# The norms' sum over partitions as one bfloat16 product instead of a float32 product

## The chip, the cores and the metric

The kernel runs on one core of a Trainium2 chip. The metric is the device time of one execution in microseconds. Before the change it was 866.14 us, the median of three runs (863.68 to 867.47).

## The reference

A random-feature attention (batch 8, 8 heads, 576 tokens, head size 64, 128 features) is followed by a bilinear feed-forward block. Cut to what matters:

```python
def phi(x):                       # x scaled by 1/sqrt(sqrt(D))
    h = einsum('bhsd,md->bhsm', x, omega) - sum(x * x, -1, keepdims=True) / 2
    return exp(h - max(h, -1, keepdims=True)) / sqrt(m)
q_p, k_p = phi(q_s), phi(k_s)
kv  = einsum('bhsm,bhsd->bhmd', k_p, v)
z   = sum(k_p, axis=2)
out = einsum('bhsm,bhmd->bhsd', q_p, kv) / (einsum('bhsm,bhm->bhs', q_p, z)[..., None] + 1e-6)
x   = out.transpose(0, 2, 1, 3).reshape(B * S, H * D)
y   = ((x @ w1) * (x @ w2)) @ w3 @ w_out
```

Everything is float32 at the interface.

## The kernel before, in words

The 4608 tokens are handled in 36 chunks of 128 tokens. Large products are done in split float16: an operand is scaled by a power of two and split into a high and a low half, and three products (high by high, high by low, low by high, the list `PASSES`) take the place of one float32 product. The power of two for a split comes from a norm, and the norms are what the change touches.

**A norm** has three steps. ScalarE squares a block and adds each partition's row up into one column of a small float32 tile (`square_sum`, L160: `sums` for the q and k chunks, `vam` for a batch of v, `wam` for W, `om_sq` for omega). TensorE multiplies this tile with a 128 by 128 matrix of ones, so that each partition holds the sum over all partitions (`power_of_two`, L165, one PSUM bank `norm_...`, 1, 3 or 8 columns). VectorE takes the exponent bits of this sum (L175), makes a power of two (L178), and its reciprocal (L180). ScalarE and VectorE then use the two to scale and split (`qhl`, `khl`, `vhl`: L143, L146).

**The stages.** For about the first 290 us the weights arrive as 64-bit words, are turned to float32 by VectorE (L500 to L504), W is made as a product of w3 and w_out (`wp`, L574 and L576), and w1, w2 and W are split. The first chunks of k and q (KF = 9 and QF = 5 of them) are projected straight in float32 (`kpj`, `qpj`, L276), the others by split float16 (L283). From then on a steady rhythm runs per chunk: the projection of q and k (`qpj`, `kpj`, L283), the attention product of a chunk (`nu`, L401), per batch the sum over keys (`kvp`, L366), the gated products (`ab`, L636, two weights, 256 tokens at a time), and the output product (`o`, L665). Every chunk of q and k that is split has one norm for both; every batch has one for v.

**What sets the order.** The order in which the parts are written comes from `step`, `put` and the loop over slots at the end (norms three slots ahead of a chunk, scale two, split one), with gate and output products taken from a queue one per slot. The framework then assigns each instruction to its engine, and every engine works through its own list in order. A line of the framework's list is one instruction; on the chip one float32 product runs as two weight loads and two matmul records, a float16 or bfloat16 product as one of each.

The matrix of float32 ones is the tile `ones` (L125, L126); a bfloat16 matrix of ones, `ones_bf` (L123, L124), already exists for the column sums of the weights' magnitudes (`l1s`, L528).

Of the kernel before, what the change touches and what calls it, by code (L numbers as in the profile page):

```python
# [9 lines left out]
F32 = mybir.dt.float32  # L10
F16 = mybir.dt.float16
BF16 = mybir.dt.bfloat16
# [7 lines left out]
P = 128  # L20
# [48 lines left out]
def tile_favor_attention_then_bilinear_ffn(  # L69
# [19 lines left out]
    nc = tc.nc  # L89
# [15 lines left out]
    const = ctx.enter_context(tc.tile_pool(name="const", bufs=1))  # L105
# [9 lines left out]
    def bank_m(name):  # L115
        return ps_m.tile([P, 512], F32, tag="pm", name=name)

    def small(name, n=1, rows=P, dt=F32, bufs=4):
        return sm.tile([rows, n], dt, tag=f"s_{name}", name=name, bufs=bufs)
# [2 lines left out]
    make_identity(nc, ident)  # L122
    ones_bf = const.tile([P, P], BF16, name="ones_bf")  # L123
    nc.vector.memset(ones_bf, 1.0)  # L124
    ones = const.tile([P, P], F32, name="ones")  # L125
    nc.vector.memset(ones, 1.0)  # L126
    ln_e = const.tile([P, 1], F32, name="ln_e")
    nc.vector.memset(ln_e, 15 * math.log(2.0))

# [32 lines left out]
    def power_of_two(cols, n, name, pre=1.0, add=False, bufs=4):  # L162

        bank = bank_m(f"norm_{name}")
        nc.tensor.matmul(bank[:, 0:n], ones, cols, start=True, stop=True)  # L165
        t = bank[:, 0:n]
        if add:
            total = small("total")
            nc.vector.tensor_reduce(total, t, AX.X, ALU.add)
            t, n = total, 1  # L170

        q = bank[:, 16 : 16 + n]
        p = bank[:, 32 : 32 + n]

        nc.vector.tensor_scalar(  # L175
            q.bitcast(I32), t.bitcast(I32), 24, 23, ALU.logical_shift_right, ALU.logical_shift_left
        )
        nc.vector.tensor_scalar(p, q, 2.0**50 / pre, 2.0**-77 / pre, ALU.mult, ALU.max)  # L178
        s = small(f"s{n}_{bufs}", n, bufs=bufs)
        nc.vector.reciprocal(s, p)  # L180
        return p, s
# [17 lines left out]
    om_sq = const.tile([P, 1], F32, name="om_sq")  # L199
    square_sum(om_sq, om_raw, "om")  # L200
    pom, som = power_of_two(om_sq, 1, "om")
    nc.scalar.mul(om[:, 0], om_raw, som)
    nc.vector.scalar_tensor_tensor(om[:, 1], om_raw, som, om[:, 0], ALU.mult, ALU.subtract)
# [29 lines left out]
    def scale(keys, am):  # L233
        p, s = power_of_two(am, 3, "_".join(f"{a}{c}" for a, c in keys), QK_PRE)
        es = small("es", 3)
        nc.vector.tensor_scalar(es, p, unom, None, ALU.mult)
        for i, k in enumerate(keys):
            scales[k] = s[:, i : i + 1], es[:, i : i + 1]
# [102 lines left out]
    def v_scale(b):  # L341
        p, sv[b] = power_of_two(vam[b], 8, f"v{b}", add=True, bufs=3)
        pv[b] = small("pv", bufs=4)
        nc.vector.tensor_scalar_mul(pv[b], p, 2.0**10)
# [370 lines left out]
    for ch in ORDER:  # L715
        n = seen.get(ch, 0)
# [95 lines left out]
    for t in range(max(plan) + 1):  # L812
        n = min(PER[t] if t < len(PER) else 1, len(ticks))
# [9 lines left out]
        n = max([1] + [-(-(k + 1) // max(due[b] - t, 1)) for k, (b, _) in enumerate(v_work)])  # L823
# [43 lines left out]
```

## Time and profile before

| what | value |
|---|---|
| median of three runs | 866.14 us |
| the profiled execution | 866.7 us |
| its span in the trace | 865.0 us |
| TensorE matmul busy | 789.3 us, 91% |
| TensorE weight loads busy | 585.1 us, 68% |
| VectorE busy | 594.4 us, 69% |
| ScalarE busy | 455.0 us, 53% |
| GpSimd busy | 222.0 us, 26% |

The span is the stretch of the trace from the first to the last instruction; 1.7 us of the profiled execution lie around it. A busy share is an average over stages, so the stage has to be looked at before an engine is called the bound. Matmuls are pipelined: the duration of one record holds its way through the array, so the cost of a product in a dense stream is read from the distance between starts, not from its duration.

### The profile page before, as it was taken

The numbers are of one execution on the slowest core, as the hardware profiler recorded it, in microseconds if no ns is written. First come the engines' busy times: TensorE is split into PE (matmuls) and PEld (weight loads), VectorE is DVE, ScalarE is ACT, GpSimd is POOL, SyncE is SP. The second block draws the span as 40 slices with busy tenths as digits, with TensorE's granted clock in tenths as the row PEclk, the third lists the DMA queues.
The fourth block names the chain that finished last, engine by engine and source line by source line (L and its number), as shares of the span: only waits on it lengthen the run. The fifth ranks groups of instructions, "written<-read, shape, count | busy, mean of one in ns | idle before, by whom it ended". The sixth has DMA issues, their size and how long they took to land.

```text
span 865.0 us, 20229 instructions
## 1 busy us (share of the span) xinstructions
PE 789.3 (91%) x8479; PEld 585.1 (68%) x8484; DVE 594.4 (69%) x1066; ACT 455.0 (53%) x813; POOL 222.0 (26%) x220
## 2 busy tenths in 40 slices
PE   2876399489996899999999999999999999999998
PEld 2344255387875777777777777877777777777774
DVE  5778887887879877777877777778777754652200
ACT  2667566758456665655565656555655443322221
POOL 0000010222333433334333334343333342222110
PEclk9996599699998999999999999999999999999999
DMA  8455646432444643644534434335342343332100
GB/s 328 150 191 164 196 129 190 119 59 62 87 112 102 96 115 95 98 75 98 123 86 87 111 98 99 74 89 133 87 87 62 62 80 81 63 62 49 37 14 36
DMA packets 142522, 88.40 MB, mean 102 GB/s; under 512 B 116704, under 2 KB 116832, under 8 KB 142432
## 3 DMA queue, kind: packets, MB, share of 16 engines
q1 hardware_dynamic: 134944, 66.15, 33.7%
q10 hardware_dynamic: 7488, 20.97, 7.3%
q8 instruction: 66, 1.08, 0.5%
q14 instruction: 24, 0.20, 0.1%
HBM read 49.35 MB, written 9.44 MB: 68 GB/s over the span
## 4 chain that ended last, share of the span: by engine, by line
PE 81%; DVE 8%; DMA 4%; ACT 4%; issue 2%; POOL 0%; SPq 0%; ACTq 0%; DVEq 0%
PE ab L636 40%; PE o L665 20%; PE wp L576 7%; PE nu L401 3%; PE kvp L366 3%; PE qpj L283 2%; PE kpj L283 2%; DMA kraw<-kT 1%; DVE nm L295 1%; DMA eqT<-eq 1%; PE wp L574 1%; DMA qraw<-qT 1%; DVE w12b L504 1%; DVE arena L503 1%; PE kpj L276 1%
## 5 line engine op out<-in xcount | busy, mean ns | idle before, releaser
L636 PE MATMUL ab<-xT,w12b 128*128 128x256 f16 (+1 forms) x3840 | 396.0, 263 | 10.4 <-DMA xT<-xhl 7.1
L636 PEld LDWEIGHTS <-w12b 128*128 128x128 f16 x3840 | 342.7, 99 | 51.7 <-issue 9.0
L665 PE MATMUL o<-Wb,arena 128*128 128x512 f16 x864 | 193.6, 379 | 1.1 <-DVE Wb L146 0.6
L651 POOL TENSOR_TENSOR arena<-asb,arena 128x512 f16<-128x512 f32 x72 | 84.5, 1174 | 294.9 <-ACT arena L650 294.4
L665 PEld LDWEIGHTS <-arena 128*128 128x128 f16 x864 | 84.3, 100 | 94.6 <-issue 1.5
L318 POOL TENSOR_TENSOR eq<-qe,eq 128x1024 f16<-128x1024 f32 x34 | 73.9, 2172 | 141.2 <-DVE eq L132 86.8
L646 DVE TENSOR_TENSOR asb<-ab,asb 128x512 f32<-128x512 f32 x72 | 49.4, 687 | 62.9 <-PE ab L636 62.5
L650 ACT CAST arena<-asb 128x512 f16<-128x512 f32 x72 | 44.3, 615 | 85.5 <-DVE asb L646 85.5
L318 POOL TENSOR_TENSOR ek<-ke,ek 128x1024 f16<-128x1024 f32 x28 | 59.7, 2131 | 103.2 <-ACT ek L134 62.2
L576 PE MATMUL wp<-w12b 128*128 128x512 f32 x128 | 60.9, 631 | 13.5 <-DVE w12b L504 13.5
L309 ACT ACTIVATE qe<-qe,ln_e,es 128x1024 f32<-128x1024 f32 x31 | 38.4, 1240 | 47.6 <-DVE qe L308 47.6
L146 DVE SCALAR_TENSOR_TENSOR khl<-kraw,s,khl 128x512 f16<-128x512 f32 x27 | 49.3, 1827 | 16.2 <-ACT khl L143 16.2
L576 PEld LDWEIGHTS wp<-w12b 128*128 128x128 f32 x128 | 25.6, 203 | 45.7 <-issue 31.3
L309 ACT ACTIVATE ke<-ke,ln_e,es 128x1024 f32<-128x1024 f32 x27 | 33.5, 1241 | 42.9 <-DVE ke L308 42.9
L146 DVE SCALAR_TENSOR_TENSOR qhl<-qraw,s,qhl 128x512 f16<-128x512 f32 x31 | 27.9, 899 | 37.7 <-ACT qhl L143 37.7
L401 PEld LDWEIGHTS <-eqT 128*128 128x128 f16 (+1 forms) x960 | 32.4, 101 | 29.0 <-DMA eqT<-eq 19.4
L401 PE MATMUL nu<-kv,eqT 128*128 128x65 f16 (+1 forms) x960 | 34.8, 196 | 18.5 <-DMA eqT<-eq 18.5
L160 ACT ACTIVATE junk_q<-qraw 128x512 bf16<-128x512 f32 x31 | 19.5, 630 | 60.4 <-DMA qraw<-qT 60.4
L645 ACT ACTIVATE asb<-ab 128x512 f32<-128x512 f32 x72 | 42.0, 584 | 16.1 <-PE ab L636 11.0
L437 ACT ACTIVATE xhl<-xs,p2r 128x512 f16<-128x512 f32 x36 | 25.9, 719 | 41.1 <-DVE p2r L189 40.1
L295 DVE TENSOR_REDUCE nm<-kpj 128x8 f32<-128x1024 f32 x36 | 43.8, 1217 | 3.6 <-PE kpj L276 3.3
L132 DVE CAST eq<-qe 128x1024 f16<-128x1024 f32 x31 | 21.5, 693 | 34.2 <-ACT qe L309 34.2
(127 smaller groups left out, 996.2 us busy)
## 6 DMA issues: line engine op xcount, KB each, us to landing
kraw<-kT SPq DMA_DIRECT2D x36, 256.0 KB, 2.7
vraw<-v SPq DMA_DIRECT2D x36, 256.0 KB, 3.5
qraw<-qT SPq DMA_DIRECT2D x36, 256.0 KB, 2.7
out<-o SPq DMA_DIRECT2D x36, 256.0 KB, 2.2
arena<-w3T ACTq DMA_DIRECT2D x8, 1024.0 KB, 5.2
arena<-w ACTq DMA_DIRECT2D x8, 1024.0 KB, 6.0
arena<-wo ACTq DMA_DIRECT2D x4, 1024.0 KB, 6.1
eqT<-eq SPq DMA_TRANSPOSE x72, 3.1
```

The costliest lines, as they stand in the source:

```text
L146: nc.vector.scalar_tensor_tensor(lo, src, s, hi, ALU.mult, ALU.subtract)
L295: nc.vector.tensor_reduce(nm, pj, AX.X, ALU.max, negate=True)
L309: nc.scalar.activation(e, e, AF.Exp, scale=es, bias=ln_e)
L318: (nc.vector if lo == "d" else nc.gpsimd).tensor_tensor(t[:, 1], e, t[:, 0], ALU.subtract)
L401: nc.tensor.matmul(nu[r0:r1, h // 4, h % 4], t[:, x, place(h), r0:r1], kvs[b][:, y, h], start=n == 0, stop=n == 2,)
L576: nc.tensor.matmul(ps, w[:, j, k * P : (k + 1) * P], guest[:, j], start=j == j0, stop=j == HALF - 1,)
L636: nc.tensor.matmul(ps[:, k], w12[m][i][cc][:, a, r * P : (r + 1) * P], x[:, b, cc, off : off + T], start=j == 0, stop=j == len(mm) - 1,)
L645: nc.scalar.mul(asb, ab[0], 2.0**-37)
L646: nc.vector.tensor_tensor(asb, ab[1], asb, ALU.mult)
L650: nc.scalar.copy(h[:, 0], asb)
L651: nc.gpsimd.tensor_tensor(h[:, 1], asb, h[:, 0], ALU.subtract)
L665: nc.tensor.matmul(ps, hs[c, f][0][:, a], W[f][:, b], start=i == 0, stop=i == len(mm) - 1)
```

## The change

The float32 matrix `ones` and its memset are gone. The sum over partitions in `power_of_two` is now a product with `ones_bf`, and the other operand is the float32 tile read as bfloat16, every second element from the second on: the upper 16 bits of each float32 word. The lower 16 bits of the sums are left out of the sum.

```diff
     ones_bf = const.tile([P, P], BF16, name="ones_bf")
     nc.vector.memset(ones_bf, 1.0)
-    ones = const.tile([P, P], F32, name="ones")
-    nc.vector.memset(ones, 1.0)
...
         bank = bank_m(f"norm_{name}")
-        nc.tensor.matmul(bank[:, 0:n], ones, cols, start=True, stop=True)
+        nc.tensor.matmul(bank[:, 0:n], ones_bf, cols.bitcast(BF16)[:, 1::2], start=True, stop=True)
```

Line numbers of the changed kernel are two lower from there on. The lists of ScalarE, GpSimd and SyncE have the same instructions in the same order; VectorE's lacks the one memset. TensorE's has one more instruction at each of the 42 norms, since a bfloat16 product is written as a weight load and a matmul.

TensorE in the steady rhythm, where the norm of q chunk 13 and k chunk 18 stands between the last projection product of a k chunk and the output products; before:

```order
L283 LDWEIGHTS khl_17_4111
L283 MATMUL kpj_17_4288<-om_87,khl_17_4111 128x128
L165 MATMUL norm_q13_k18_4321<-sums_1_103,ones_80 128x3
L665 LDWEIGHTS arena_111
L665 MATMUL o_6_4335<-Wb_84,arena_111 128x512
```

and with the change:

```order
L281 LDWEIGHTS khl_17_4109
L281 MATMUL kpj_17_4286<-om_85,khl_17_4109 128x128
L163 LDWEIGHTS ones_bf_78
L163 MATMUL norm_q13_k18_4319<-sums_1_101,ones_bf_78 128x3
L663 LDWEIGHTS arena_109
L663 MATMUL o_6_4333<-Wb_82,arena_109 128x512
```

The place in the list is the same; the one row has become two.

TensorE at the start, where the norm of omega stands among the eight float32 products of the first k chunk; before:

```order
L862 UNCONDITIONAL_BRANCH
L276 MATMUL kpj_0_139<-Wb_84,kraw_0_114 128x128 x3
L165 MATMUL norm_om_91<-om_sq_88,ones_80 128x1
L276 MATMUL kpj_0_139<-Wb_84,kraw_0_114 128x128 x5
L276 MATMUL kpj_1_209<-Wb_84,kraw_1_116 128x128 x8
```

and with the change:

```order
L860 UNCONDITIONAL_BRANCH
L274 MATMUL kpj_0_137<-Wb_82,kraw_0_112 128x128 x3
L163 LDWEIGHTS ones_bf_78
L163 MATMUL norm_om_89<-om_sq_86,ones_bf_78 128x1
L274 MATMUL kpj_0_137<-Wb_82,kraw_0_112 128x128 x5
L274 MATMUL kpj_1_207<-Wb_82,kraw_1_114 128x128 x8
```

Here too the place is the same. Besides the norms, two neighbouring pairs have changed places in TensorE's list: two `ab` products with each other, and four `ab` products with one `kvp` product of the same batch.

## Rows read from the trace of the kernel before

**Rows 1.** Windows: us, then busy of each engine, granted clock, DMA share, GB/s.

```profile
90.00:100.00 10.00, 1.88 (x14) 1.49 (x14) 9.91 (x12) 8.11 (x18) 0.00 (x0) 0.50 0.48 117
...
289.00:400.00 111.00, 111.00 (x1342) 87.05 (x1343) 84.31 (x153) 63.35 (x107) 40.78 (x44) 0.98 0.49 99
```

**Rows 2.** TensorE's waits from 289 us to the end.

```profile
PE kvp L366 <- DVE ke L308: 2.8, 1, 2.8
```

**Rows 3.** Instructions on the tile `ones`: durations min/median/max, first and last start.

```profile
L165 PE MATMUL norm_q_k<-sums,ones x52: 168/252/273, 202.6 to 672.0; 128*128 128x3 f32 x52
...
L126 DVE MEMSET ones<- x1: 165/165/165, 1.0 to 1.0; 128x128 f32 x1
```

**Rows 4.** TensorE in order of time, in pieces: start, us, what.

```profile
305.61 0.84 PE L283 MATMUL kpj<-om,khl 64*128 64x128 f16 x24
306.39 0.38 PE L165 MATMUL norm_q_k<-sums,ones 128*128 128x3 f32 x2
306.63 3.61 PE L665 MATMUL o<-Wb,arena 128*128 128x512 f16 x16
...
348.80 0.90 PE L401 MATMUL nu<-kv,eqT 128*128 128x65 f16 x24
349.54 5.41 PE L636 MATMUL ab<-xT,w12b 128*128 128x256 f16 x48
354.88 0.84 PE L283 MATMUL qpj<-om,qhl 64*128 64x128 f16 x24
355.65 5.41 PE L636 MATMUL ab<-xT,w12b 128*128 128x256 f16 x48
...
367.93 3.79 PE L366 MATMUL kvp<-vhl,ek 128*128 128x65 f16 x120
...
407.85 0.90 PE L401 MATMUL nu<-kv,eqT 128*128 128x65 f16 x24
...
408.81 5.40 PE L636 MATMUL ab<-xT,w12b 128*128 128x256 f16 x48
...
690.28 0.38 PE L165 MATMUL norm_q<-sums,ones 128*128 128x3 f32 x2
```

**Rows 5.** The same view late: `ab` to `o` with (norm left out) and without a norm.

```profile
702.55 5.41 PE L636 MATMUL ab<-xT,w12b 128*128 128x256 f16 x48
...
707.94 5.34 PE L665 MATMUL o<-Wb,arena 128*128 128x512 f16 x24
...
776.10 5.41 PE L636 MATMUL ab<-xT,w12b 128*128 128x256 f16 x48
781.35 5.34 PE L665 MATMUL o<-Wb,arena 128*128 128x512 f16 x24
```

**Rows 6.** The chain that ended last, before 290 us, in order of time: start, us, what.

```profile
8.34 0.52 PE norm_om L165 x2
...
105.29 8.79 PE wp L576 x16
...
115.17 7.06 PE wp L576 x16
122.24 5.36 PE ab L636 x96
...
136.97 0.20 PE norm_v L165 x2
...
180.26 0.17 PE norm_k L165 x2
...
223.73 0.12 PE norm_q_k L165 x2
```

**Rows 7.** The same chain later: the `kvp` products of one batch.

```profile
368.09 3.63 PE kvp L366 x120
```

**Rows 8.** Weight loads of bfloat16 ones: shape, count, busy us, mean ns, idle before.

```profile
L528 PEld LDWEIGHTS <-ones_bf 128*128 128x128 bf16 x16 | 1.3, 110 | 1.3 <-issue 1.0
```

**Rows 9.** VectorE in order of time: the reading that sets a `kpj` bank free.

```profile
364.00 1.23 DVE L308 TENSOR_TENSOR ke<-kpj,nm 128x1024 f32<-128x1024 f32 x1
```

## The prediction

> **What bounds the kernel now.** The windows by stage come first. From 90 to 100 us TensorE is busy for 1.88 of 10 us at a granted clock of 0.50, while VectorE is busy for 9.91; from 289 to 400 us TensorE is busy for all of 111 us, VectorE for 84.31 and ScalarE for 63.35 [rows 1]. So there are two kernels in one: before about 290 us a chain that goes from engine to engine, after it one in which TensorE does not rest. The waits confirm the second: from 289 us to the end TensorE waits once, for 2.8 us, and this is the wait for the `kvp` products that opens the stretch [rows 2]. Whatever TensorE does not have to do after it is time won, as long as the other engines keep up; before it, only what lies on the chain counts.
>
> Next comes what a norm costs there, and a record's duration misleads. The 26 joint norms of q and k alone are 52 matmul records with a median of 252 ns [rows 3]; that is the way through the array, much of which lies beside the neighbours. I therefore compare the distance between the starts of what stands before and behind, with a norm and without.
>
> - Between `kpj` and `o`: from the first `kpj` to the first `o` it is 306.63 - 305.61 = 1.02 us; the equal 24 products of `qpj` hand over to `ab` after 355.65 - 354.88 = 0.77 us without a norm [rows 4]. The norm costs 0.25 us. This happens 21 times, first with the norm at 306.39 us and last with that at 690.28 us [rows 4].
> - Between `nu` and `ab`: 408.81 - 407.85 = 0.96 us with the norm of v, 349.54 - 348.80 = 0.74 us without [rows 4]. It costs 0.22 us, 5 times.
> - Between `ab` and `o`, late, where only q is left: 707.94 - 702.55 = 5.39 us with, 781.35 - 776.10 = 5.25 us without [rows 5]. It costs 0.14 us, 4 times: the longer `ab` products cover part of the float32 weight load.
>
> Together 21 x 0.25 + 5 x 0.22 + 4 x 0.14 = 6.9 us of the dense stretch are norms. The other 12 of the 42 norms stand before 290 us, and four of them show on the chain: 0.52, 0.20, 0.17 and 0.12 us [rows 6], together 1.0 us.
>
> **The change part by part.** *The float32 product goes.* This takes away 6.9 us after 290 us and at most 1.0 us before.
>
> *A bfloat16 pair comes in its place*, one weight load and one product of at most 8 columns. No row shows such a pair among others. The nearest are pairs of the same full weight load with a float16 product of 65 columns: 120 `kvp` products take 3.63 us [rows 7], so 30 ns for a pair. I take 0.03 us for each of the 30, 0.9 us in all. The bounds: nothing, since a pair inserted in a full stream cannot take less; and 0.11 us, a whole weight load of bfloat16 ones laid bare [rows 8], 3.3 us in all. The 30 ns are nearer because the load in the `kvp` stream has as little cover as here.
>
> A pair with a longer product is dearer: 96 `ab` products of 128 columns take 5.36 us, 56 ns for a load and a product [rows 6]. Against my price stands the Trainium skill, page "TensorE: Matmul & The Clock Gate", section "Back-to-back issue gap": a stream of weight loads and products of 128 columns is said to sustain about 81 ns for a pair. This case's trace does not agree, with 56 ns for the same pair. By the page's figure an estimate for the new pairs is 30 x 0.081 = 2.4 us, and the whole gain would be 5.0 us instead of the 6.5 us below.
>
> *The dense stretch* wins 6.9 - 0.9 = 6.0 us, with bounds of 3.6 and 6.9.
>
> *The stretch before 290 us.* The norm of omega is the one that matters: its 0.52 us lie straight on the chain, between the first float32 `kpj` and VectorE's work on the first weights. The other three are short, and transfers and waits behind them may swallow what they give. With new pairs of 0.03 us, and 0.06 us for the first, at most 1.0 - 0.15 = 0.85 us are won. I take 0.5 us, about what the norm of omega gives, and keep 0 and 0.85 as ends.
>
> *The result comes sooner*, by some tenths of a microsecond. I count nothing for it in the dense stretch, where no TensorE work waits for VectorE [rows 2].
>
> *The memset goes*, 165 ns at 1.0 us [rows 3]; the first norm starts at 8.34 us [rows 6], so its cover is wide, and without it the cost would be those 165 ns once. The truncated sums may turn a power of two by one step now and then; no instruction depends on its value. *The two exchanged pairs* of TensorE's list move products of 30 to 56 ns past each other before 290 us; nothing.
>
> *Nothing new is waited for.* The pair waits for the squares as the float32 product did. What is queued behind it on TensorE (`o` or `ab`) starts sooner; it reads operands made a step earlier. What is late next is a PSUM bank: `kvp` at 367.93 us takes the bank that VectorE sets free at 364.00 + 1.23 = 365.23 us [rows 4, 9], 2.7 us ahead, and the change brings TensorE forward by about 0.2 us in a step of 18 us, with VectorE at three quarters of its time.
>
> **Sum.** 6.0 + 0.5 = 6.5 us. The profiled execution took 866.7 us (a span of 865.0 and 1.7 around it), so it would take 860.2 us. The median of the runs is 0.56 us lower, 866.14 us, and becomes **859.6 us**, 0.75% less.
>
> **The rivals.**
>
> 1. *The pair costs more than 30 ns*, since its load and the load behind it find only a product of a few columns to hide beside. At the 56 ns of an `ab` pair [rows 6] 30 of them cost 1.7 us, the gain is 6.9 - 1.7 + 0.5 = 5.7 us and the time 860.4 us; with a whole load of 0.11 us bare and nothing won early it is 3.6 us and 862.5 us. For it speaks that no row has a bfloat16 pair so short; against it, that even the long float32 loads are partly covered behind `ab`. The page named above lies between the two, at 861.1 us.
> 2. *The early stretch takes a different turn.* TensorE's clock is granted at 0.50 (1.2 GHz, the lower of its two levels) where it stood still most [rows 1]. Sixteen equal `wp` products took 8.79 us when they began behind such a wait and 7.06 us a little later [rows 6]: 1.7 us for one burst more at the lower level. One burst gives 861.3 us, two 863.0; one less gives 857.9. For it: shifts of tenths before 100 us reach a clock that changes there; against it: no wait there hangs on a norm for longer than 0.5 us.
> 3. *The gain is swallowed by another engine*, 866.1 us. Against it stand the 2.7 us of slack and VectorE's 84.31 us of 111 [rows 1, 9].
> 4. *Slower: the stream drains at each change of type.* If the bfloat16 load could begin only once the float16 products had left the array, and the next float16 load only once the norm had left it, load, product and next load would stand in series: 0.11 + 0.25 + 0.11 = 0.47 us with the durations of [rows 3, 8], 14.1 us for 30 against 6.9 removed, and 873.3 us with nothing won early. It turns into a loss from 0.23 us a norm. Against it: the float32 norm is such a change of type too, and costs 0.14 to 0.25 us with two loads and two products.
> 5. *The list promises one load and one product, the chip makes two of each as for float32.* Then nothing changes, 866.1 us. Against it: the bfloat16 ones for the weights' magnitudes have 16 loads for 16 listed products [rows 8].
>
> **How the numbers follow.** My forecast 0.58; the dearer pair 0.20, most of it below 861.8 us; the early stretch 0.10; swallowed 0.08; slower 0.03; two of each 0.01. A measurement of this kernel can tell about 0.5%, or 4.3 us, from no change: faster is below 861.8 us. The runs before lie up to 2.5 us from their median, so about a tenth of the forecast's own chance falls above that line, as do four tenths of the dearer pair, half of the early turn and the swallowed gain. Faster 0.69, within 0.5% 0.28, slower 0.03. The range: the free pair with all of the early gain gives 866.14 - 6.9 - 0.85 = 858.4 us, and a little over a microsecond for the scatter of a median leads to 857.2; upward it takes in the bare load and reaches 863.4.
>
> **What would show it.** Right: 42 matmul records and 42 weight loads on the norm's line instead of 84 each; 0.80 us in place of 1.02 from the first `kpj` to the first `o`, and about 5.28 in place of 5.39 from `ab` to `o`; TensorE without waits after its dense stretch has begun; that stretch about 6 us shorter, and its begin less than 1 us earlier. Wrong: new TensorE waits in it (rival 3), a distance from `kpj` to `o` above 0.85 us (rival 1) or above 1.0 us (rival 4), or a begin of the stretch that moved by more than 1 us either way (rival 2).

## The result and the profile after

The changed kernel takes 858.09 us in the median of five runs (856.64 to 861.15), against 866.14 us before. The ratio is 0.9914 with a 95% interval of 0.9886 to 0.9943, a gain of 7.4 us (4.9 to 9.9). A second measurement of the same kernel (`again`, below) gives 859.03 us and a ratio of 0.9929 (0.9910 to 0.9948), a gain of 6.1 us (4.5 to 7.8). Forecast were 859.6 us and a gain of 6.5.

The windows of the changed kernel, with the columns of [rows 1]:

```profile
90.00:100.00 10.00, 1.88 (x14) 1.49 (x14) 8.52 (x11) 6.42 (x15) 0.00 (x0) 0.50 0.67 181
289.00:400.00 111.00, 111.00 (x1296) 84.78 (x1293) 84.42 (x150) 61.35 (x103) 40.25 (x45) 1.00 0.48 97
```

There are still two stages: TensorE without a pause in the dense stretch and at 1.88 of 10 us near 95 us. VectorE has 84.42 us of 111, so no engine has come close to the bound. TensorE's waits from 275 us to the end, which answer to [rows 2]:

```profile
PE kvp L364 <- DVE ke L306: 2.9, 1, 2.9
PE kpj L281 <- DVE khl L144: 1.6, 1, 1.6
```

Only the opening wait lies in the dense stretch; the other stood before it already, outside the window of [rows 2]. No new wait has come. The instructions on `ones_bf` at the norms, which answer to [rows 3]:

```profile
L163 PEld LDWEIGHTS <-ones_bf x42: 95/96/105, 8.2 to 753.7; 128*128 128x128 bf16 x42
L163 PE MATMUL norm_q_k<-sums,ones_bf x26: 167/178/178, 199.0 to 662.5; 128*128 128x3 bf16 x26
```

For 26 joint norms there are 26 matmul records where there were 52, and 42 weight loads in all where there were 84. TensorE in order of time, which answers to [rows 4, 5]:

```profile
301.04 0.84 PE L281 MATMUL kpj<-om,khl 64*128 64x128 f16 x24
301.82 0.18 PE L163 MATMUL norm_q_k<-sums,ones_bf 128*128 128x3 bf16 x1
301.86 5.34 PE L663 MATMUL o<-Wb,arena 128*128 128x512 f16 x24
307.03 0.90 PE L399 MATMUL nu<-kv,eqT 128*128 128x65 f16 x24
307.77 0.17 PE L163 MATMUL norm_v<-vam,ones_bf 128*128 128x8 bf16 x1
307.80 2.45 PE L634 MATMUL ab<-xT,w12b 128*128 128x256 f16 x21
...
692.76 5.41 PE L634 MATMUL ab<-xT,w12b 128*128 128x256 f16 x48
698.01 0.17 PE L163 MATMUL norm_q<-sums,ones_bf 128*128 128x3 bf16 x1
698.04 5.34 PE L663 MATMUL o<-Wb,arena 128*128 128x512 f16 x24
```

This is where the time went. From the first `kpj` to the first `o` it is 0.82 us where it was 1.02; from `nu` to `ab` 0.77 where it was 0.96; from `ab` to `o` 5.28 where it was 5.39. A norm's record still lasts 0.17 to 0.18 us, but the product behind it starts 0.03 to 0.04 us after it: the duration of a record is not what it costs.

For the dense stretch a fixed mark is needed. I take the start of the first norm in it (q 11, k 16) and the end of the span: 865.0 - 306.39 = 558.6 us before [rows 4], 854.7 - 301.82 = 552.9 us after. TensorE's granted clock is 1.00 (2.4 GHz, the higher of its two levels) from the mark to the end in both. So 5.7 us come from the dense stretch. The other 4.6 us by which this execution's span is shorter lie ahead of the mark, and the experiments show that most of them are no effect of the change.

### The profile page after: what moved, and what is told of

Same layout as the page of the kernel before. It is cut to its first block, busy times and chain, and to the rows that moved or that the text cites. A ratio compares the mean times of both kernels' runs of the same rounds, so it can differ in the third digit from the quotient of the medians.

```text
span 854.7 us, 20148 instructions
## 1 busy us (share of the span) xinstructions
PE 780.3 (91%) x8442; PEld 575.7 (67%) x8442; DVE 594.4 (70%) x1065; ACT 455.5 (53%) x813; POOL 221.6 (26%) x220
## 4 chain that ended last, share of the span: by engine, by line
PE 82%; DVE 7%; DMA 5%; ACT 4%; issue 1%; POOL 0%; SPq 0%; ACTq 0%; DVEq 0%
PE ab L634 41%; PE o L663 20%; PE wp L574 7%; PE nu L399 3%; PE kvp L364 3%; PE qpj L281 3%; PE kpj L281 2%; DMA qraw<-qT 2%; DMA eqT<-eq 1%; DVE nm L293 1%; DMA arena<-wo 1%; PE qpj L274 1%; DVE arena L501 1%; PE wp L572 1%; DVE w12b L502 1%
## 5 line engine op out<-in xcount | busy, mean ns | idle before, releaser
L663 PEld LDWEIGHTS <-arena 128*128 128x128 f16 x864 | 82.2, 98 | 94.8 <-issue 1.8
```

The source lines that it names most:

```text
L663: nc.tensor.matmul(ps, hs[c, f][0][:, a], W[f][:, b], start=i == 0, stop=i == len(mm) - 1)
```

## The experiments

My theory: each norm of the dense stretch gives back TensorE's time for a float32 product, less a cheap pair, and the early stretch adds half a microsecond and a scatter of its own. The main rival: norms that are ready sooner speed the early stretch up for good.

**The late norms alone, and the early norms alone** (`late`, `early`). `FIRST` holds the names of the first 12 norms; `early` has `in` for `not in`.

```diff
-        nc.tensor.matmul(bank[:, 0:n], ones, cols, start=True, stop=True)
+        if name not in FIRST:
+            nc.tensor.matmul(bank[:, 0:n], ones_bf, cols.bitcast(BF16)[:, 1::2], start=True, stop=True)
+        else:
+            nc.tensor.matmul(bank[:, 0:n], ones, cols, start=True, stop=True)
```

> The float32 ones stay for the first 12 norms (omega, v 0 to 2, W, k 9, and the joint norms up to q 10 and k 15); the 30 norms of the dense stretch use the bfloat16 product. Theory (the gain is TensorE's time in the dense stretch): 6.0 us less than before, and in the trace the stretch from the opening kvp products to the end is 570.0 us as in the changed kernel, against 576.0 before. Rival (the gain comes from norms that are ready sooner in the early stretch): 3 to 4 us less than before at most, with a dense stretch near 573.

> The reverse: the first 12 norms use the bfloat16 product, the 30 of the dense stretch the float32 one. Theory: 0.5 us less than before (0 to 0.85), with a dense stretch of 576.0 us. Rival (early norms are worth more than their place on the chain): 2 us less than before or more, with the dense stretch beginning 2 to 4 us sooner in every execution.

`late` took 859.75 us, a ratio of 0.9939 (0.9916 to 0.9962) to its runs of before: 5.3 us less (3.3 to 7.3), where 6.0 were expected. `early` took 863.75 us, 0.9987 (0.9973 to 1.0001): 1.1 us less, with an interval from 2.3 less to 0.1 more, where 0.5 were expected. Together they make 6.4 us, between the 7.4 and the 6.1 us measured for the whole change. The mark in their traces, first that of `late`:

```profile
304.86 0.18 PE L167 MATMUL norm_q_k<-sums,ones_bf 128*128 128x3 bf16 x1
304.90 5.34 PE L669 MATMUL o<-Wb,arena 128*128 128x512 f16 x24
```

and that of `early`:

```profile
301.77 0.39 PE L169 MATMUL norm_q_k<-sums,ones 128*128 128x3 f32 x2
302.01 5.34 PE L669 MATMUL o<-Wb,arena 128*128 128x512 f16 x24
```

From the mark to the end `late` needs 857.8 - 304.86 = 552.9 us, the value of the change, and `early` 860.4 - 301.77 = 558.6 us, that of before. The rival expected at most 4 us for `late`, with a dense stretch about 3 us longer. The interval of the runs alone would let it stand; the dense stretch does not, and it falls.

The expectations count from the opening `kvp` products and not from the mark. In order of the lines: before, changed, `early`, `again` (below).

```profile
288.97 5.35 PE L366 MATMUL kvp<-vhl,ek 128*128 128x65 f16 x120 [2.81 <-DVE ke L308]
284.74 5.00 PE L364 MATMUL kvp<-vhl,ek 128*128 128x65 f16 x120 [2.91 <-DVE ke L306]
285.90 3.80 PE L370 MATMUL kvp<-vhl,ek 128*128 128x65 f16 x120 [2.63 <-DVE ke L312]
288.94 3.80 PE L364 MATMUL kvp<-vhl,ek 128*128 128x65 f16 x120 [2.98 <-DVE ke L306]
```

The same 120 products take 5.35 and 5.00 us where the granted clock was 0.72 (six microseconds from 288 us before, from 284 us changed), and 3.80 us where it was 1.00. Counted from here the stretch is 576.0 us before, 570.0 changed, 570.2 in `late`, 574.5 in `early` and 568.8 in `again`: where that misses the expectations of 576.0 and 570.0, the miss is the clock of these first products.

The rival of `early` is harder to dismiss. Its profiled execution does reach the dense stretch 3.1 us sooner than before, as that rival wanted. Against it stand the twelve runs, with 1.1 us, though their interval just reaches the rival's 2 us, and `again`, which has the same early norms and begins at 288.94 us.

**The changed kernel once more** (`again`).

> The changed kernel once more, to see how far its early stretch scatters. Theory: 7 to 8 us less than before; the dense stretch takes 570.0 us again, while its begin lies anywhere from 284 to 288 us. Rival (the early gain is fixed): the begin lies at 284.7 us again within 0.5.

Its runs gave 6.1 us (4.5 to 7.8) less than before, below the 7 to 8 us that I expected. Its profiled execution took 859.61 us, against 856.64 of the first. The dense stretch is the same, 857.7 - 304.81 = 552.9 us, but the mark lies at 304.81 us instead of 301.82, and the opening `kvp` start at 288.94 instead of 284.74 us, slightly later even than I had allowed. So one and the same kernel reaches the dense stretch 4.2 us apart, which is as much as the first profiled execution seemed to have won there (288.97 to 284.74 us); the fixed early gain of the rival falls. At the mark 3.0 us of it are left, since the opening `kvp` products took 1.2 us less in `again`. A large part of it is seen in the chain between 90 and 106 us, first of the changed kernel:

```profile
93.79 7.05 DMA eqT<-eq
...
103.67 2.93 PE wp L574 x3
```

then of the same kernel in `again`:

```profile
93.52 9.50 DMA eqT<-eq
...
105.85 1.22 PE wp L574
```

The transposing transfer of the first q chunk starts 0.27 us sooner and takes 2.45 us longer; the `wp` products behind it start 2.2 us later. The rest is added in pieces up to 289 us. In the other traces the same transfer takes from 6.91 us (before) to 9.59 us (`double32`), both with float32 norms, so its length does not go by the norms.

**The bfloat16 product three times** (`triple16`).

```diff
-        nc.tensor.matmul(bank[:, 0:n], ones_bf, cols.bitcast(BF16)[:, 1::2], start=True, stop=True)
+        for _ in range(3):
+            nc.tensor.matmul(bank[:, 0:n], ones_bf, cols.bitcast(BF16)[:, 1::2], start=True, stop=True)
```

> Every norm issues its bfloat16 product three times into the same bank. Theory (a pair costs 30 to 40 ns in the stream): two more pairs at 42 norms, in the dense stretch 30 x 2 x 0.035 = 2.1 us more than the changed kernel, and the distance from kpj to o grows from 0.82 to about 0.89 us. Rival (a bare weight load, 0.11 us a pair): 6.6 us more, 1.04 us from kpj to o.

TensorE at the mark:

```profile
305.24 0.84 PE L282 MATMUL kpj<-om,khl 64*128 64x128 f16 x24
306.02 0.23 PE L164 MATMUL norm_q_k<-sums,ones_bf 128*128 128x3 bf16 x3
306.11 5.34 PE L664 MATMUL o<-Wb,arena 128*128 128x512 f16 x24
```

From `kpj` to `o` it is 0.87 us, 0.05 more for two more pairs, or 25 ns a pair; from the mark to the end 860.4 - 306.02 = 554.4 us, 1.5 us more for 60 pairs, 25 ns again, somewhat less than the 30 to 40 ns that I expected. A bare weight load would have shown 6.6 us. The runs, 858.82 us and a ratio of 0.9924 (0.9906 to 0.9942), can't show 1.5 us beside `again`: its interval and this one overlap almost wholly. Here the distance in the trace decides, not the median.

**The float32 product twice** (`double32`, made from the kernel before).

```diff
         nc.tensor.matmul(bank[:, 0:n], ones, cols, start=True, stop=True)
+        nc.tensor.matmul(bank[:, 0:n], ones, cols, start=True, stop=True)
```

> The kernel before, with every float32 norm product issued twice into the same bank. Theory (a float32 norm holds TensorE for 0.22 to 0.25 us of a full stream, and what it holds is paid in full): the 30 norms of the dense stretch add 30 x 0.22 to 0.25, 6.6 to 7.5 us, and the early ones 0 to 1, so 7 to 8 us more than before, with 1.25 us from kpj to o. Rival (another engine is close behind TensorE and takes up changes of this size): 3 us or less.

It took 873.6 us, a ratio of 1.0077 (1.0054 to 1.0100): 6.7 us more than before (4.7 to 8.7). At the mark:

```profile
306.57 0.84 PE L284 MATMUL kpj<-om,khl 64*128 64x128 f16 x24
307.34 0.39 PE L165 MATMUL norm_q_k<-sums,ones 128*128 128x3 f32 x2
307.59 0.36 PE L166 MATMUL norm_q_k<-sums,ones 128*128 128x3 f32 x2
307.81 5.34 PE L666 MATMUL o<-Wb,arena 128*128 128x512 f16 x24
```

From `kpj` to `o` it is 1.24 us, as expected. The second product adds 0.22 us from start to start, and as much between `ab` and `o` (714.71 to 714.93 us), where the first costs 0.14. From the mark to the end it is 872.6 - 307.34 = 565.3 us, 6.7 more than before for 30 norms. What a float32 norm holds of TensorE there is paid in full; nothing takes it up.

**No product at all** (`nosum`), which failed as a measure of the floor.

```diff
-        nc.tensor.matmul(bank[:, 0:n], ones_bf, cols.bitcast(BF16)[:, 1::2], start=True, stop=True)
-        t = bank[:, 0:n]
+        t = cols
```

> The norms' product is left out altogether: VectorE makes the power of two from each partition's own sum of squares, so the sum over partitions is missing and the output is not the reference's. It gives the floor for any form of the sum on TensorE. Theory (a pair costs 30 to 40 ns): the stretch from the same kpj to the end is 1.1 us shorter than in the changed kernel (30 x 0.035), the hand-over from kpj to o 0.78 us. Rival (the pair's cost is hidden, 0): no shorter than in the changed kernel within 0.3 us.

It took 891.21 us, 25.6 us more than before by the ratio of 1.0296 (1.0279 to 1.0313). VectorE's list came out in another order without the step on TensorE, and from 300 to 700 us TensorE now waits:

```profile
PE kvp L363 <- DVE ke L305: 19.8, 4, 5.3
```

So the experiment changed more than it was meant to, and its time says nothing on the pair. Only the hand-over can be used:

```profile
323.00 0.84 PE L280 MATMUL kpj<-om,khl 64*128 64x128 f16 x24
323.78 5.35 PE L662 MATMUL o<-Wb,arena 128*128 128x512 f16 x24
```

`o` follows on the first `kpj` after 323.78 - 323.00 = 0.78 us, 0.04 less than in the changed kernel, so the pair's cost is not hidden.

**TensorE kept busy before the first `wp`** (`warm`). This asks whether the early scatter is one of the clock, and whether there is more to win.

```diff
                 ps = bank_m(f"wp_{n}_{k}")
+                if n == 0 and k == 0:
+                    for _ in range(15):
+                        warm = guest[:, 0].bitcast(BF16)[:, 1::2]
+                        nc.tensor.matmul(ps, ones_bf, warm, start=True, stop=True)
```

> The changed kernel, with 15 products of 512 columns (ones by the first converted block of w_out, into the bank that the first wp product then overwrites) in TensorE's long wait before the first wp product. If the early stretch scatters because TensorE begins the 48 wp products at the lower clock: they take 21.2 us instead of 22.3 to 23.7, and 1 to 2 us less than the changed kernel come out. Rival (transfers set the end of the early stretch): the wp products are as much shorter, but the dense stretch begins no sooner than at 284 to 289 us, and the time is that of the changed kernel.

TensorE in order of time, `warm`:

```profile
17.00 5.28 PE L574 MATMUL wp<-w12b,ones_bf 128*128 128x512 bf16 x15 [5.17 <-DVE w12b L502]
24.70 20.87 PE L578 MATMUL wp<-w12b 128*128 128x512 f32 x48 [2.43 <-DVE w12b L502]
...
70.09 1.22 PE L274 MATMUL qpj<-Wb,qraw 64*128 64x128 f32 x6 [2.75 <-ACT ke L304]
```

and the changed kernel:

```profile
24.27 22.72 PE L574 MATMUL wp<-w12b 128*128 128x512 f32 x48 [12.89 <-DVE w12b L502]
...
70.25 1.22 PE L274 MATMUL qpj<-Wb,qraw 64*128 64x128 f32 x6 [1.98 <-ACT ke L304]
```

The 48 products are 1.85 us shorter, and end 1.4 us sooner. At 70 us the lead is down to 0.16 us: `qpj` waits for ScalarE there, 2.75 us instead of 1.98. Then the transposing transfer takes 8.31 us, against 7.05 in the changed kernel:

```profile
93.64 8.31 DMA eqT<-eq
```

The opening `kvp` start at 288.38 us, and the runs give 860.42 us, 0.9938 (0.9920 to 0.9956), no better than the changed kernel. They still lie from 857.53 to 862.29 us, as wide apart as those of the changed kernel (856.64 to 861.15). The rival holds: at 70 us ScalarE has taken most of the lead back, and the transfer takes more than the rest. I found no version that beats the change.

The marks side by side, all from the first dense norm to the end of the span:

| kernel | dense norms | mark, us | span, us | mark to end, us |
|---|---|---|---|---|
| before | float32 | 306.39 | 865.0 | 558.6 |
| early | float32 | 301.77 | 860.4 | 558.6 |
| double32 | float32 twice | 307.34 | 872.6 | 565.3 |
| changed | bfloat16 | 301.82 | 854.7 | 552.9 |
| again | bfloat16 | 304.81 | 857.7 | 552.9 |
| late | bfloat16 | 304.86 | 857.8 | 552.9 |
| warm | bfloat16 | 304.25 | 857.1 | 552.9 |
| triple16 | bfloat16 three times | 306.02 | 860.4 | 554.4 |

The last column goes by the kind of the product alone, to a tenth of a microsecond, at a granted clock of 1.00. The mark scatters: two traces of the changed kernel lie 3.0 us apart, and the kernels with float32 norms in the early stretch (before, `late`, `double32`: 304.86 to 307.34 us) overlap with the others (301.77 to 306.02). Single traces can't show what the early norms give.

## Why the prediction was right

*What bounds the kernel.* Right: TensorE without a pause after 290 us, and `double32` shows that its time there is paid one for one.

*The price of the float32 norm.* Right: 6.9 us were read from hand-overs; the 5.7 us won and the 1.1 us of the new pairs (below) make 6.8. `double32` adds 6.7 us for one more at each place, 0.22 us also where the first costs 0.14. That fits the forecast's reading that the long `ab` products cover part of the first.

*The price of the pair.* Right in kind and a little low. Forecast were 0.03 us; measured are 0.04 us between `kpj` and `o` and 0.03 at the other places, 21 x 0.04 + 9 x 0.03 = 1.1 us instead of 0.9. That, and differences of two starts that are good to a hundredth, make 5.7 us of the forecast 6.0. The Trainium skill, page "TensorE: Matmul & The Clock Gate", section "Back-to-back issue gap", gives its 81 ns for pairs with 128 columns. The prediction's estimate of 2.4 us from it for the short pairs is not borne out, with 1.1 us measured and 25 ns for one more pair in `triple16`. The same page of the Trainium skill says in its section "Wait — 56ns, not 53.3ns?" that the distance of two starts never falls below about 25 ns however few the columns. The additional pairs of `triple16` sit at that value.

*The early stretch.* Forecast was 0.5 us, and `early` measures 1.1 with an interval from -0.1 to 2.3. The place is as forecast. The first `wp`, before and in `early`:

```profile
25.00 23.41 PE L576 MATMUL wp<-w12b 128*128 128x512 f32 x48 [12.86 <-DVE w12b L504]
24.39 22.93 PE L580 MATMUL wp<-w12b 128*128 128x512 f32 x48 [12.87 <-DVE w12b L508]
```

It starts at 25.00 and 24.86 us with omega's norm in float32 (before, `late`) and at 24.27, 24.39 and 24.20 us in bfloat16 (changed, `early`, `again`), some 0.6 us sooner. How much of it reaches 290 us, the scatter of some 4 us hides; that stays open.

*The sum.* 6.5 us, against 7.4 (4.9 to 9.9) and 6.1 (4.5 to 7.8) us in two measurements. The two differ by the kernel before and not by the change: the changed kernel took 858.8 and 858.9 us in the mean of their runs, the kernel before 866.2 and 864.9. The first profiled execution of the changed kernel was the fastest of its five runs, so its early stretch flatters the change. That the sum lands so near is in part luck: the dense term came out 0.3 us below the forecast, and the early one is known no better than to a microsecond.

*The rivals.* The dearer pair is excluded by `triple16`, draining at each change of type by the hand-over of 0.82 us (above 1.0 was wanted), swallowing by the 5.7 us of the dense stretch itself and by `double32`, and two of each by the count of records. The sign of rival 2 did appear: the begin of the dense stretch moved by 4.2 us, and more than 1 us was to speak against the forecast. The sign was badly chosen, since `again`, the same kernel, begins at 288.94 us, where the kernel before does (288.97). The early stretch does take different turns, but for the same kernel too, and by transfers as well as by the clock that I had blamed.

## What to carry to other kernels

A float32 product of a few columns costs a dense TensorE stream some 0.14 to 0.25 us, for its two weight loads and two matmul records (0.22 to 0.25 us behind products of 65 and 128 columns, 0.14 us behind products of 256), and a 16-bit pair 0.03 to 0.04 us; where only an exponent is read from the sum, the upper half of the float32 word is enough and needs no conversion. Price a step by the distance between its neighbours' starts, with it and without, never by its record's duration. Where a kernel has a stretch that scatters by more than the change is worth, measure from a mark behind it, and take one part of the change at a time before believing that the rest of a gain is real.

## What the runs showed of the hardware

VectorE's subtraction for a split takes very different times by what GpSimd does beside it. In the changed kernel, VectorE's two splits of one step in order of time:

```profile
345.78 0.75 DVE L144 SCALAR_TENSOR_TENSOR qhl<-qraw,s,qhl 128x512 f16<-128x512 f32 x1 [1.52 <-ACT qhl L141]
347.34 2.10 DVE L144 SCALAR_TENSOR_TENSOR khl<-kraw,s,khl 128x512 f16<-128x512 f32 x1 [0.81 <-ACT khl L141]
```

and GpSimd's subtraction beside the second:

```profile
346.76 2.13 POOL L316 TENSOR_TENSOR ek<-ke,ek 128x1024 f16<-128x1024 f32 x1 [2.63 <-ACT ek L132]
```

The same form takes 0.75 us alone and 2.10 us when GpSimd works, and ends 0.55 us after GpSimd has ended (349.44 against 348.89). Between 300 and 700 us of this trace 23 such operations begin while GpSimd is at work, and whether they take 0.74 or 2.11 us, each ends 0.54 to 0.56 us after it; 49 with no GpSimd operation beside them take 0.74 or 0.75 us. In `nosum` the order is turned round: there `qhl` meets GpSimd and takes 2.35 us, from 326.85 to 329.20, while GpSimd works from 326.52 to 328.64, again 0.56 us after its end. It looks as if VectorE's operation made little way until GpSimd had finished; no run here was made to test that. A new order on VectorE thus changes which operations are held up; how much of the longer time of `nosum` comes from that is not shown.
